# Moving the first four chunks' state updates of a fused linear-attention and ELU-MLP kernel into the second half of the first tile

## The chip, the cores and the metric

The kernel runs on one core of one Trainium2 chip. The metric is the device time of one execution in microseconds; the time of a version is the median of several executions.

## The reference

Decayed causal linear attention in blocks, for 4 batches, 8 heads, 768 positions and a head dimension of 64, followed by a two-layer network on the 3072 tokens of 512 features, with 2048 hidden features and ELU between the layers. Inputs and output are float32. Cut to what matters:

```python
for b in range(nb):                                   # blocks of the sequence
    intra = (qb @ kb.T * Dmask) @ vb                  # Dmask[i, j] = lam ** (i - j), i >= j
    inter = (qb * lam_pow) @ kv_state
    out[block b] = intra + inter
    kv_state = lam_block * kv_state + (kb * rev_pow).T @ vb
...
h = x @ w_in                                          # x: the heads of a token side by side
g = np.where(h > 0, h, np.exp(np.minimum(h, 0)) - 1)
y = g @ w_out
```

## The kernel before

The kernel uses blocks of 128 positions rather than 64. A chunk is one such block of one batch: with 6 blocks and 4 batches there are 24 chunks, numbered g = 4c + b. Chunks 0 to 3 are the first block of each batch, which have no state to read. The MLP runs over seven tiles of 4, 2, 4, 4, 4, 4 and 2 chunks (128 tokens per chunk), so tile 0 is chunks 0 to 3 (512 tokens).

Everything is ordered by hand (`manual_schedule`): the order in which the Python code emits instructions is the order of each engine's queue, and each engine works through its queue in order, waiting on what the tile framework finds it depends on.

For a chunk the attention part has these steps. `att_T` and `att_Te` transpose q and k on TensorE and copy them out (later chunks use a DMA transpose instead). `att_S` makes the score products into psS, `att_mask` multiplies them with the decay mask on VectorE into P (L323), `att_O` makes the output products from P and v (L337) and from q and the state (L345), and `att_X` writes the result as the MLP's input xt. For the state there are `att_kd`, the key decay kd = k times the per-head factors (L298 on VectorE or GpSimd, L296 on ScalarE), for two chunks at once; `att_U`, the update products from kd and v into psU (L383, 16 small matmuls for a pair of chunks); and `att_st`, which brings psU into the state st: for chunks 0 to 3 two plain copies per pair (L417, VectorE), later eight multiply-adds per pair (L421). So kd0, U0, st0 stand for chunks 0 and 1, and kd2, U2, st2 for chunks 2 and 3. The first reader of these states is `att_O` of chunks 4 and 5, at step B7, and of chunks 6 and 7.

The MLP has steps named (tile, n). `mm1` makes hidden feature block n of a tile, four matmuls into psH (L444), then exp into e (L473) and relu into r (L477) on ScalarE; `elu` combines them on VectorE into g (L490). For n = 2, 4 and 6 of tile 0 the relu is left out and VectorE does two instructions instead, m from e (L485) and g from m and psH (L488). `mm2` is one output product for one chunk of the tile and one block n, accumulated in psM (L541), copied out after n = 15 (L555, L557) and stored by SyncE's queue.

Tile 0 is special. Its 16 hidden blocks are steps A0 to A15; from A10 on each also holds two output products, of chunks 0 and 1. Steps B0 to B12 hold the other output products of tile 0, and between them the attention of chunks 4 to 7 (`visit`): chunk 4's transposes and kd4 at B1, its scores at B4, its output products at B7. Within a step the order is: `mm1`, then whatever `at` has put on this step, then `elu`, then the `mm2` of the step.

PSUM tiles are taken from tags with two slots each: "H" and "M" for psH and psM (in tile 0, the psH of even n below 9 use "M"), "S" for psT, psS, psO and psU. A new tile takes the slot of the tile before the last one of its tag, and its first writer waits until that tile has been read. The SBUF tags e and r have three slots, kd has two.

All loads with a cast from float32 to float16 are issued by GpSimd's queue, in the order of the list LOADS: q, k and v of the first chunks, then the slices wi0 to wi7 of W_in (128 KB each for wi0 and wi1, 256 KB for wi2 to wi6, 512 KB for wi7), the slices wo0 to wo4 of W_out (256 KB each for wo0 and wo1, else 512 KB), and q, k and v of later chunks in pairs. The entries ('kd', g) of the list are no loads: GpSimd itself computes kd of chunks g and g + 1 at that place of its queue. wi0 and wi1 hold hidden blocks 0 and 1, wi2 to wi6 blocks 2 to 11 in pairs, wi7 blocks 12 to 15; wo0 holds hidden blocks 0 and 1 for the second layer, wo1 blocks 2 and 3, wo2 to wo4 the rest in fours.

Of the kernel before, what the change touches and what calls it, by code (L numbers as in the profile page):

```python
# [15 lines left out]
def kernel(  # L16
# [12 lines left out]
    B, H, S, D = q.shape  # L29
# [82 lines left out]
        [cpool.tile([128, 2, HP, 128], FP16, name=f"st{j}_{i}") for i in range(2)]  # L112
        for j in range(B // 2)
    ]
    LOADS = [(0, 1, 'q'), (0, 1, 'k'), (1, 1, 'q'), (1, 1, 'k'), (2, 1, 'q'), (2, 1, 'k'), (3, 1, 'q'), (3, 1, 'k'), (0, 1, 'v'), (1, 1, 'v'), (2, 1, 'v'), (3, 1, 'v'), ('wi', 0), ('wi', 1), ('wi', 2), ('wi', 3), ('wi', 4), ('kd', 0), ('wi', 5), ('wi', 6), ('wo', 0), ('wi', 7), ('kd', 2), ('wo', 1), ('wo', 2), (4, 2), ('wo', 3), ('wo', 4), (6, 2), (8, 2), (10, 2), (12, 2), (14, 2), (16, 2), (18, 2), (20, 2), (22, 2)]

    def run_loads(items):
        for it in items:
            if it[0] == "wi":
                emit_wi(it[1])  # L120
            elif it[0] == "wo":
                emit_wo(it[1])
            elif it[0] == "kd":
                att_kd(it[1], 2, "p")
            else:
                emit_load(*it)

    run_loads(LOADS[:0])
    nc.gpsimd.iota(rel_i[:], pattern=[[1, 128]], base=0, channel_multiplier=-1)
    run_loads(LOADS[0:16])  # L130

# [447 lines left out]
    def at(s, f, *a, **k):  # L579
        run.setdefault(s, []).append(lambda: f(*a, **k))  # L580
# [66 lines left out]

    run_loads(LOADS[16:29])
    for s, g in zip([], (0, 2)):
        at(s, att_kd, g, 2)  # L650
    for s, g in zip([('A', 6), ('A', 9)], (0, 2)):
        at(s, att_U, g)
    for s, g in zip([('A', 7), ('A', 10)], (0, 2)):
        at(s, att_st, g)
        at(s, att_tmp, g + B)

# [39 lines left out]
    for s, a, b in [(('B', 2), 29, 30), ((1, 2), 30, 31), ((1, 14), 31, 32), ((2, 4), 32, 33), ((2, 12), 33, 34), ((3, 4), 34, 35), ((3, 12), 35, 36), ((4, 4), 36, 37)]:  # L696
        at(s, paced_load, s, LOADS[a:b])

# [51 lines left out]
```

## Time and profile before

| what | value |
|---|---|
| median of 7 executions | 212.71 us (212.54 to 213.73) |
| the profiled execution | 213.73 us, of which the span is 212.0 us |
| TensorE, matmuls busy | 201.9 us (95% of the span) |
| VectorE busy | 148.7 us (70%) |
| ScalarE busy | 127.1 us (60%) |
| GpSimd busy | 62.4 us (29%) |
| granted TensorE clock | 1.00 |
| steps A0 to A15 of tile 0 | 18.05 to 36.76 us of the span |
| kd of chunks 0, 1 and of 2, 3 on GpSimd | start 15.67 and 20.54, 2.05 and 2.16 us |
| U of chunks 0, 1 and of 2, 3 on TensorE | start 25.36 and 28.43 |
| state copies L417 on VectorE | start 28.50 and 31.86, two each, 0.69 us per copy |

The span runs from the first to the last instruction; the rest of an execution's time lies around it. A busy share is an average over stages with different limits, so the stages are looked at one by one. The TensorE clock was never throttled, so a difference in time is one of work or of waiting. All times inside the span are counted from its start.

### The profile page before, as it was taken

Reading aid. Unit: us, or ns where it says so; the run is one execution under the profiler, and the core shown is the slowest. Engines: PE = TensorE matmul, PEld = TensorE weight load, DVE = VectorE, ACT = ScalarE, POOL = GpSimd, SP = SyncE. Lnnn points to the kernel's source line nnn. Section 1 sums busy time; section 2 is a strip of 40 time slices with the busy share of each in tenths; the row PEclk is TensorE's granted clock in tenths of the full one; section 3 lists DMA queues with packets and bytes.
Section 4 is the critical chain, followed back from the end, with each engine's and each line's share of the span. In section 5 each row is a group of like instructions: output and inputs, shape, how many; then the busy total and the mean of one; then the engine's idle time right before and its main releaser. Section 6 shows DMA issues by size and latency. Waiting matters only on the chain.

```text
span 212.0 us, 4131 instructions
## 1 busy us (share of the span) xinstructions
PE 201.9 (95%) x1640; PEld 104.6 (49%) x1640; DVE 148.7 (70%) x241; ACT 127.1 (60%) x246; POOL 62.4 (29%) x71
## 2 busy tenths in 40 slices
PE   6786899999999999999999999999999999999994
PEld 2343344555865454544544544544544544466643
DVE  7662998477989999998698598677557634344321
ACT  5885778505694858666464666464567476675520
POOL 8999985400343352150600510600000000011000
PEclk9999999999999999999999999999999999999999
DMA  6999999999999999999699791599401111011112
GB/s 42 141 152 182 196 195 166 197 157 195 189 149 134 132 170 156 143 87 114 113 143 144 119 132 52 111 144 154 90 0 53 49 49 49 2 53 49 49 53 101
DMA packets 101284, 24.40 MB, mean 115 GB/s; under 512 B 93072, under 2 KB 98448, under 8 KB 101264
## 3 DMA queue, kind: packets, MB, share of 16 engines
q0 software_dynamic: 80912, 14.16, 86.6%
q1 hardware_dynamic: 20208, 9.90, 21.7%
q8 instruction: 13, 0.21, 0.4%
q10 hardware_dynamic: 144, 0.07, 0.1%
q14 instruction: 7, 0.06, 0.1%
HBM read 27.27 MB, written 6.29 MB: 158 GB/s over the span
## 4 chain that ended last, share of the span: by engine, by line
PE 79%; DVE 7%; POOL 5%; ACT 4%; DMA 3%; issue 1%; POOLq 0%; ACTq 0%
PE psM L541 36%; PE psH L444 28%; PE psH L462 5%; DVE g L490 3%; DMA wi<-in_moe_w_in_dram 3%; PE psO L337 2%; PE psS L311 2%; PE psO L345 2%; POOL qn L74 2%; POOL kn L74 2%; PE psM L521 2%; POOL vn L74 2%; ACT r L477 2%; DVE P L323 1%; ACT kd L296 1%
## 5 line engine op out<-in xcount | busy, mean ns | idle before, releaser
L541 PE MATMUL psM<-wo,g 128*128 128x512 f16 x368 | 94.0, 380 | 0.2 <-DVE g L490 0.2
L473 ACT ACTIVATE e<-psH 128x512 f32<-128x512 f32 x96 | 57.3, 598 | 61.4 <-PE psH L444 51.5
L490 DVE SCALAR_TENSOR_TENSOR g<-e,r 128x512 f16<-128x512 f32 x93 | 63.9, 702 | 38.2 <-ACT r L477 37.8
L444 PE MATMUL psH<-xt,wi 128*128 128x512 f16 (+2 forms) x324 | 81.2, 376 | 2.9 <-DMA wi<-in_moe_w_in_dram 1.7
L477 ACT ACTIVATE r<-psH 128x512 f16<-128x512 f32 x93 | 55.2, 594 | 0.0
L541 PEld LDWEIGHTS <-g 128*128 128x128 f16 x368 | 34.3, 98 | 38.5 <-DVE g L490 1.5
L444 PEld LDWEIGHTS <-wi 128*128 128x128 f16 x324 | 31.1, 98 | 40.8 <-DMA wi<-in_moe_w_in_dram 2.4
L323 DVE TENSOR_TENSOR P<-psS,mask 128x1024 f16<-128x1024 f32 (+1 forms) x28 | 28.7, 1066 | 5.7 <-PE psS L311 5.6
L691 POOL COPY pace<-g 1x1 f16<-1x1 f16 x7 | 2.3, 329 | 70.5 <-DVE g L490 70.5
L421 DVE SCALAR_TENSOR_TENSOR st<-st,up_p,psU 64x128 f16<-64x128 f16 x64 | 18.2, 346 | 0.1
L558 POOL DMA_DIRECT2D out_dram<-osb x2 | 1.1, 572 | 54.8 <-ACT osb L557 50.7
L366 DVE TENSOR_TENSOR xt<-psO,qs 128x1024 f16<-128x1024 f32 x10 | 12.2, 1223 | 6.7 <-PE psO L345 6.7
L462 PE MATMUL psH<-xt,wi 128*128 128x256 f16 x128 | 16.4, 273 | 0.0
L74 POOL DMA_DIRECT2D qn<-in_q_dram x14 | 15.3, 1092 | 3.2 <-issue 2.0
L74 POOL DMA_DIRECT2D kn<-in_k_dram x14 | 15.2, 1087 | 1.3 <-DMA kn<-in_k_dram 0.8
L74 POOL DMA_DIRECT2D vn<-in_v_dram x14 | 15.2, 1104 | 1.1 <-DMA wo<-in_moe_w_out_dram 1.1
L462 PEld LDWEIGHTS <-wi 128*128 128x128 f16 x128 | 12.3, 98 | 4.2
L557 ACT COPY osb<-psM 128x512 f32<-128x512 f32 x12 | 7.1, 592 | 12.2 <-PE psM L541 12.2
L337 PEld LDWEIGHTS <-vn 128*64 128x64 f16 x184 | 9.6, 109 | 4.9 <-issue 3.8
L337 PE MATMUL psO<-P,vn 128*64 128x128 f16 x184 | 11.5, 222 | 0.2
L345 PE MATMUL psO<-qT,st 128*64 128x128 f16 x160 | 10.0, 219 | 0.0
L345 PEld LDWEIGHTS <-st 128*64 128x64 f16 x160 | 8.9, 110 | 0.0
(58 smaller groups left out, 112.8 us busy)
## 6 DMA issues: line engine op xcount, KB each, us to landing
out_dram<-osb SPq DMA_DIRECT2D x21, 256.0 KB, 2.5
qn<-in_q_dram POOLq DMA_DIRECT2D x10, 256.0 KB, 6.9
kn<-in_k_dram POOLq DMA_DIRECT2D x10, 256.0 KB, 7.7
vn<-in_v_dram POOLq DMA_DIRECT2D x10, 256.0 KB, 9.0
wo<-in_moe_w_out_dram POOLq DMA_DIRECT2D x3, 512.0 KB, 13.1
wi<-in_moe_w_in_dram POOLq DMA_DIRECT2D x5, 256.0 KB, 7.0
qn<-in_q_dram POOLq DMA_DIRECT2D x4, 128.0 KB, 4.3
kn<-in_k_dram POOLq DMA_DIRECT2D x4, 128.0 KB, 4.3
```

The source lines that it names most:

```text
L74: nc.gpsimd.dma_start(out=dst, in_=src[b : b + n, :, rows].rearrange("b h p d -> p (b h) d"))
L323: nc.vector.tensor_tensor(out=P[:, :, c], in0=s[:, :, c], in1=(mask if g < B else mask1)[:, :, c], op=ALU.mult,)
L337: nc.tensor.matmul(po[r, i, hp, :], lhsT=v_of(g + i, 2 * hp + hh), rhs=P[:, hh, hp, :], start=True, stop=(c == 0), skip_group_check=True,)
L345: nc.tensor.matmul(po[r, i, hp, :], lhsT=st[(g + i) % B // 2][c % 2][:, (g + i) % 2, hp, r], rhs=qT[g + i][:, hp, :], start=False, stop=Tr ...
L366: nc.vector.tensor_tensor(out=dst, in0=po[:, :, c], in1=qs[:, c].unsqueeze(1).broadcast_to([128, n, w, 128]), op=ALU.mult,)
L421: nc.vector.scalar_tensor_tensor(out=new[r, :, hp, r], in0=old[r, :, hp, r], scalar=up_p[r, hp : hp + 1], in1=pu[r, :, hp, :], op0=ALU.mul ...
L444: nc.tensor.matmul(pH[:, lo:hi], lhsT=wi[:, kk, j * 128 : (j + 1) * 128], rhs=xt[t][:, kk, lo:hi], start=(kk == 0), stop=(kk == HP - 1),)
L462: nc.tensor.matmul(pH[:, x * MT : (x + 1) * MT], lhsT=wi[:, kk, j * 128 : (j + 1) * 128], rhs=xt[t][:, kk, :], start=(kk == 0), stop=(kk = ...
L473: nc.scalar.activation(e[:], pH[:], AF.Exp)
L477: nc.scalar.activation(r[:], pH[:], AF.Relu)
L490: nc.vector.scalar_tensor_tensor(out=g, in0=e[:], scalar=-1.0, in1=r[:], op0=ALU.add, op1=ALU.min)
L541: nc.tensor.matmul(pm[:], lhsT=gt[t][:, n, i * L : (i + 1) * L], rhs=wo_t[wo_at[n][0]][:, wo_at[n][1], :], start=(n == 0), stop=(n == NF - 1),
```

## The change

Three things move, none is added or removed. In LOADS, the two key decays on GpSimd go behind the last slice of W_in: kd0 from behind wi4 to behind wi7, and kd2 from behind wi7 to behind wo1. With this wi7 comes ahead of wo0. The update products go from A6 and A9 to B0 and B2, and the state copies from A7 and A10 to B1 and B3. The calls of `att_tmp` that go along do nothing in this version.

```diff
-    LOADS = [..., ('wi', 4), ('kd', 0), ('wi', 5), ('wi', 6), ('wo', 0), ('wi', 7), ('kd', 2), ('wo', 1), ('wo', 2), (4, 2), ...]
+    LOADS = [..., ('wi', 4), ('wi', 5), ('wi', 6), ('wi', 7), ('kd', 0), ('wo', 0), ('wo', 1), ('kd', 2), ('wo', 2), (4, 2), ...]
...
-    for s, g in zip([('A', 6), ('A', 9)], (0, 2)):
+    for s, g in zip([('B', 0), ('B', 2)], (0, 2)):
         at(s, att_U, g)
-    for s, g in zip([('A', 7), ('A', 10)], (0, 2)):
+    for s, g in zip([('B', 1), ('B', 3)], (0, 2)):
         at(s, att_st, g)
         at(s, att_tmp, g + B)
```

More of the change, by code (lines that the diff above doesn't have):

```diff
@@ L114 @@
     ]
-    LOADS = [(0, 1, 'q'), (0, 1, 'k'), (1, 1, 'q'), (1, 1, 'k'), (2, 1, 'q'), (2, 1, 'k'), (3, 1, 'q'), (3, 1, 'k'), (0, 1, 'v'), (1, 1, 'v'), (2, 1, 'v'), (3, 1, 'v'), ('wi', 0), ('wi', 1), ('wi', 2), ('wi', 3), ('wi', 4), ('kd', 0), ('wi', 5), ('wi', 6), ('wo', 0), ('wi', 7), ('kd', 2), ('wo', 1), ('wo', 2), (4, 2), ('wo', 3), ('wo', 4), (6, 2), (8, 2), (10, 2), (12, 2), (14, 2), (16, 2), (18, 2), (20, 2), (22, 2)]
+    LOADS = [(0, 1, 'q'), (0, 1, 'k'), (1, 1, 'q'), (1, 1, 'k'), (2, 1, 'q'), (2, 1, 'k'), (3, 1, 'q'), (3, 1, 'k'), (0, 1, 'v'), (1, 1, 'v'), (2, 1, 'v'), (3, 1, 'v'), ('wi', 0), ('wi', 1), ('wi', 2), ('wi', 3), ('wi', 4), ('wi', 5), ('wi', 6), ('wi', 7), ('kd', 0), ('wo', 0), ('wo', 1), ('kd', 2), ('wo', 2), (4, 2), ('wo', 3), ('wo', 4), (6, 2), (8, 2), (10, 2), (12, 2), (14, 2), (16, 2), (18, 2), (20, 2), (22, 2)]
     def run_loads(items):
```

## The prediction

> **What bounds the kernel now.** I read the page's first part, then the table of busy time by stretches, then the chain that ended last, then the timelines of the engines around the moved work.
>
> ```profile
> PE 201.9 (95%) x1640; PEld 104.6 (49%) x1640; DVE 148.7 (70%) x241; ACT 127.1 (60%) x246; POOL 62.4 (29%) x71
> ```
>
> TensorE is busy 95% of the span, so only places where it waits can be won. Stretches of 4 us (start:end, length, then busy us of PE, PEld, DVE, ACT, POOL):
>
> ```profile
> 22.00:26.00 4.00, 3.20 (x30) 1.39 (x29) 3.93 (x6) 3.19 (x6) 4.00 (x5) 1.00 1.31 195
> 30.00:34.00 4.00, 3.72 (x18) 1.56 (x16) 3.92 (x7) 3.15 (x6) 2.46 (x3) 1.00 2.03 170
> 38.00:42.00 4.00, 4.00 (x45) 2.31 (x42) 1.83 (x3) 1.93 (x2) 1.42 (x2) 1.00 1.41 196
> 42.00:46.00 4.00, 4.00 (x65) 2.34 (x62) 2.42 (x3) 0.00 (x0) 0.00 (x0) 1.00 2.41 158
> ```
>
> In the first half of tile 0 (steps A) VectorE is full and TensorE has gaps; in the second half (steps B, from about 37 us) TensorE is full and VectorE half idle. The chain says the same (start, us, what):
>
> ```profile
> 21.23 2.02 DVE g L490
> ...
> 27.89 0.69 DVE g L488
> 28.58 0.59 DVE st L417
> 29.20 0.69 DVE st L417
> 29.93 0.70 DVE g L490
> ...
> 31.31 0.50 ACT r L477
> 31.85 1.02 PE psH L444 x4
> ...
> 36.76 1.29 PE psM L541 x6
> 38.05 0.89 PE psT L224 x16
> ...
> 41.54 0.55 PE psS L311 x16
> 42.09 2.70 PE psM L541 x12
> ```
>
> From 21.23 to 30.63 it runs through VectorE, a state copy (L417) in it, and from 31.85 to 57.77 through TensorE without a break.
>
> ```profile
> 20.54 2.16 POOL L298 TENSOR_TENSOR kd<-kn,ks 128x1024 f16<-128x1024 f16 x1
> 24.41 1.02 PE L444 MATMUL psH<-xt,wi 128*128 128x512 f16 x4 [0.80 <-DVE g L488]
> 37.91 0.69 DVE L490 SCALAR_TENSOR_TENSOR g<-e,r 128x512 f16<-128x512 f32 x1 [0.60 <-ACT r L477]
> ```
>
> The g of 21.23 takes 2.02 us instead of 0.69 and ends 0.55 after GpSimd's kd; the wait of step A6 at 24.41 is its consequence.
>
> **What the Trainium skill says.** "SBUF — State Buffer", section "Who interferes with whom": a VectorE instruction with two SBUF inputs contends with a GpSimd instruction that reads SBUF, one in a two-port mode with any GpSimd instruction; the first to issue holds the pair for its whole instruction. The trace agrees: g (L490, e and r both in SBUF) took 2.02 us beside kd, and m (L485, one SBUF source) 0.40, 0.63 and 0.97 us in the chain, the longer two while GpSimd issued loads. "DMA: Bandwidth & Descriptors", section "Queues, rings and completion order": within a ring, descriptors are consumed in order. The landings of the weights agree, below.
>
> **The change part by part.**
>
> *GpSimd's order.* After wi4 (15.67) came kd0, wi5, wi6, wo0, wi7, kd2, wo1; now wi5, wi6, wi7, kd0, wo0, wo1, kd2. One weight load takes 0.70 to 0.79 us there, kd0 1.85 from its start to that of the next. So kd0 starts at 15.67 + 0.77 + 0.77 + 0.79 = 18.0 and wo0 at 19.85, before VectorE's first g (20.25): kd0 stays free. kd2 starts at 19.85 + 0.70 + 0.76 = 21.3, hence beside the second g (21.23 to 21.92). It waits for that, then holds the pair to about 23.55; m2, queued behind g1, waits for it. Then m2 ends at 23.95, g2 at 24.6 (24.36 before). The lock moves from g1 to m2 and costs 0.25 us here. Bounds: if m2 gets in ahead of kd2, g2 ends at 23.05, but g3, with two SBUF inputs, is blocked instead; if kd2 lingers, g2 ends at 24.75.
>
> *The weights' landings.* Issue to landing was 7.5 us for wo0 (19.05) and 9.4 for wi7 (19.75):
>
> ```profile
> wi<-in_moe_w_in_dram POOLq DMA_DIRECT2D x1, 512.0 KB, 9.4
> wo<-in_moe_w_out_dram POOLq DMA_DIRECT2D x1, 256.0 KB, 7.5
> ```
>
> So the landings were wi5 23.9, wi6 25.3, wo0 26.55, wi7 29.15, wo1 30.35: about 1.3 us for each 256 KB, a backlog served in order. Issuing earlier brings nothing; order does. Now wi7 lands at 25.3 + 2.6 = 27.9 (nobody needs it before A12) and wo0 at 29.15. The first output product (psM, step A10) started at 29.68: from 29.2 on wo0 is its floor. wo1 (30.4) and wo2 (32.9) stay ahead of their users; k4 landed at 36.7, and its transposes still come after that.
>
> *State copies (L417).* Four by 0.69 us leave VectorE's queue in A. g7, which ended at 30.63, now ends near 29.4, so exp and relu (ACT) at A10 no longer wait, and A12's wait goes. What is late next is A11's buffer (relu of A9, behind m6) and wo0. With the first output product at 29.2 to 29.35, TensorE's own work from there to the end of A15 is 5 first-layer groups plus the A10 to A14 output pairs: 5 x 0.864 + 5 x 0.43 = 6.48 us. A15 ends at 35.7; with a wait of 0.3 at A11 at 36.0. Before: 36.76. **Gain 0.74 to 1.06 us; I take 0.95.**
>
> *Update products (L383).* In A they lay beside TensorE's waits; in B nothing covers them. Each is 0.25 us in the chain at 45.80, and 0.37 from start to the next start in A (28.43 to 28.80). Two: 0.5 to 0.74; I take **0.6 lost**.
>
> *VectorE and the PSUM slots in B.* Tag "S" has two slots. The order was U0, U2, T4, S4, S5; it is now U0, T4, U2, S4, S5. So U2 needs st0 done and S5 needs st2 done. Counted from A15's end: VectorE's last g ends at 38.60 - 36.76 = 1.84; st0 (1.40 for its pair) 3.24; kd4 (L298, 1.22) 4.46; st2 5.86. TensorE reaches U2 at 0.43 + 0.25 + 0.86 + 0.89 + 0.86 = 3.29, hardly late, and S5 at 3.29 + 0.25 + 0.86 + 0.86 + 0.28 = 5.54. S5 waits until about 5.92: **0.4 lost**, with all TensorE work behind it. Bounds: 0 if U's longer 0.37 delays TensorE by as much, 0.6 if a copy is slowed. The mask of chunk 5 ends at about 8.3, and O(5) comes at about 9.2: covered. kd4's slot needs U0 only, long done. The two DVE copies as such (2.8 us) lie in VectorE's idle time in B. SP's queue and GpSimd's loads in B stay in their order.
>
> *Sum:* -0.95 + 0.6 + 0.4 = +0.05 us. The profiled execution took 213.73 us with a span of 212.0, thus 1.73 around it and 1.02 over the median; I put the sum on the median: **212.7 us**. The ends of the terms, with U's two prices tied to S5's wait, give -0.25 to +0.6.
>
> **The rivals.** About 0.64 us (0.3%) is what a measurement of this kernel can tell from no change.
>
> *B swallows the moved work (faster).* If S5 doesn't wait on st2 and the update products cost nothing net, the gain of A stays: 212.71 - 1.06 = 211.65; with the products paid, 212.1. For it: VectorE is under half busy from 38 to 42. Against: TensorE's chain has no gap there for 0.5 us of added products. Chance of more than 0.64: 0.18.
>
> *wo0 decides at A10 (slower).* wo0 is now issued at 19.85 behind 512 KB more. If it lands later than 29.15, every later tenth comes off A's gain, as A11 stands behind it on TensorE and nothing after A10 waits elsewhere. At 30.2 the gain is gone: 30.2 + 6.48 = 36.7. Then products and S5's wait remain, 1.0 lost: 213.7. The limit of 0.64 is passed from 29.85 on. Against it: the even landings. For it: a landing of 10.3 us after issue is in the range of what other loads of the queue show (wo1 7.7, wo2 9.5, k4 11.4). The same 1.0 would follow if kd2's lock put m2 so late that A6 starts near 25.5. Together 0.28.
>
> *It doesn't do what it says:* if kd2 didn't collide at all, VectorE would lead in A, but wo0's floor keeps the gain at 1.06, so this changes only 0.1 us.
>
> **How the numbers follow.** Nothing measurable 0.54, faster 0.18, slower 0.28. The likeliest case's own range is 212.45 to 213.3; to leave out 1 in 10 at either end it stretches to the faster rival without its extreme, 211.9, and to the slower one, 213.8.
>
> **What would show each step.** Right: TensorE's gap before A12 gone; one m (L485) near 2 us in place of the long g, or a g3 of that length; wo0 landing near 29.2, with the first psM product just after; A15 ending near 35.8; a new wait of psS (L311) on st (L417) of about 0.4 us near 41.5; chunk 4's and 5's O products (L337) at the same time as before, 44.8, within 0.5. Wrong: a wait of L541 on the wo load well beyond 29.5, a wait at the first psO of B, or a TensorE chain of B that starts earlier by 1 us and stays so.

## The result, and the profile after

The changed kernel takes 213.86 us in the median of 13 executions (213.62 to 214.71), the kernel before 212.61 us in the median of 34. The ratio is 1.0061, with a 95% interval of 1.005 to 1.0073: about 1.3 us slower.

The two profiled executions don't show this: the span was 212.0 us before and 211.9 after. The execution of the kernel before that was profiled had taken 213.73 us, 1.1 over its own median, while the one profiled after (213.71) was as long as its timed ones. A second profile of the kernel before took 213.93 us; a third, with 212.67 us and a span of 210.8, has the usual length. It is called "before, third profile" here, and the changed kernel is compared with it.

The engines' totals after, from the page:

```profile
PE 203.4 (96%) x1640; PEld 105.5 (50%) x1640; DVE 150.6 (71%) x241; ACT 127.4 (60%) x246; POOL 62.5 (29%) x71
```

Three of the stretches of 4 us shown of before, now after (start:end, length, busy us of PE, PEld, DVE, ACT, POOL):

```profile
22.00:26.00 4.00, 2.73 (x13) 1.17 (x12) 3.93 (x5) 2.75 (x6) 4.00 (x4) 1.00 1.32 204
30.00:34.00 4.00, 4.00 (x20) 1.86 (x19) 2.51 (x4) 3.45 (x8) 2.46 (x3) 1.00 2.11 170
38.00:42.00 4.00, 4.00 (x53) 2.06 (x50) 3.63 (x6) 1.93 (x2) 1.63 (x2) 1.00 1.48 195
```

The same stretches of before, third profile (two of them):

```profile
22.00:26.00 4.00, 3.93 (x33) 1.71 (x31) 3.93 (x7) 3.13 (x6) 4.00 (x5) 1.00 1.31 199
30.00:34.00 4.00, 4.00 (x20) 1.82 (x19) 3.90 (x7) 3.66 (x8) 2.44 (x3) 1.00 2.00 167
```

The change did what it set out to do: VectorE has room from 30 to 34 us (2.51 against 3.90 busy) and takes the copies in from 38 to 42. But in a usual execution of the kernel before TensorE was not short of work from 30 to 34: it was full at 4.00. And from 22 to 26 it now works 2.73 us in place of 3.93. The chain that ended last, after (start, us, what):

```profile
18.86 2.83 DVE g L490 x2
21.70 2.05 DVE m L485
...
23.77 0.70 DVE g L488
...
24.52 4.64 PE psH L444 x20
29.15 0.55 PE psM L541 x2
...
35.78 0.43 PE psM L541 x2
36.21 0.37 PE psU L383 x16
36.59 0.97 PE psM L541 x4
37.55 0.89 PE psT L224 x16
38.45 0.86 PE psM L541 x4
39.31 0.37 PE psU L383 x16
39.68 1.83 PE psM L541 x8
41.52 0.55 PE psS L311 x16
```

And of before, third profile:

```profile
21.63 1.22 DVE m L485
...
23.62 1.02 PE psH L444 x4
24.65 0.37 PE psU L383 x16
25.02 2.70 PE psH L444 x12
27.71 0.37 PE psU L383 x16
28.09 0.97 PE psH L444 x4
...
35.56 1.29 PE psM L541 x6
36.86 0.89 PE psT L224 x16
37.75 2.59 PE psM L541 x12
40.34 0.55 PE psS L311 x16
```

Both chains hang on m2 (L485) until step A6, and then on TensorE without a break up to chunk 4's scores (psS), 40.34 before and 41.52 after: 1.18 us. This is made up as follows.

- A6 starts 0.90 later (24.52 against 23.62).
- The two update products are no longer in A. Each took 0.37 us there, and the group behind it 0.11 more than its matmuls alone (2.70 for 12 of them against 12 x 0.216 = 2.59, 0.97 for 4 against 4 x 0.216 = 0.86): 0.95 less for both.
- TensorE waits 0.27 more in A: 0.16 in the 20 matmuls from A6 on (4.64, against 1.02 for the first four and 16 x 0.216 = 3.46 for the rest), and 0.1 at A10's two output products (0.55 for the two, elsewhere 0.43). So A15 ends 0.22 later (35.78 against 35.56).
- In B the products are 0.37 each again, and the output products behind each take 0.11 and 0.10 more (0.97 against 0.86, 1.83 against 8 x 0.216 = 1.73): 0.95.

The sum is 0.22 + 0.95 = 1.17. The products cost the same in both places, so moving them comes to nothing. What the change costs is A6's 0.90 and the 0.27 of waiting behind it. The spans differ by 1.1.

The two waits after A6, in the timelines of VectorE and of TensorE's weight loads (PEld), after:

```profile
25.66 0.69 DVE L488 TENSOR_TENSOR g<-m,psH 128x512 f16<-128x512 f16 x1
26.40 2.25 PEld L444 LDWEIGHTS <-wi 128*128 128x128 f16 x11 [0.28 <-issue]
29.09 0.11 PEld L541 LDWEIGHTS <-g 128*128 128x128 f16 x2 [0.43 <-DMA wo<-in_moe_w_out_dram]
```

The psH of A8 takes the slot of A4's, which g4 (L488) reads until 26.35; A8 starts right behind it. With the products gone from A, TensorE has caught up with the late VectorE. At A10 the weight load waits for wo0 until 29.09. TensorE was still at work for most of that wait, so it cost 0.1.

Why A6 is late, in the timelines of VectorE and GpSimd (start, us, engine, line, operation), first before, third profile, then after:

```profile
20.54 2.01 POOL L298 TENSOR_TENSOR kd<-kn,ks 128x1024 f16<-128x1024 f16 x1
21.63 1.21 DVE L485 TENSOR_SCALAR m<-e 128x512 f16<-128x512 f32 x1 [0.89 <-ACT e L473]
```

```profile
21.21 2.24 POOL L298 TENSOR_TENSOR kd<-kn,ks 128x1024 f16<-128x1024 f16 x1
21.62 2.12 DVE L485 TENSOR_SCALAR m<-e 128x512 f16<-128x512 f32 x1
```

m2 starts at the same time in both, which is a coincidence: before, it waited for e, and after, for the two g ahead of it, the first of which took 2.23 us. It takes 0.42 us when nothing holds it; it ends 0.29 us after GpSimd's kd2 in each. kd2 ends at 22.55 before and 23.45 after, and this 0.90 is A6's delay.

### The profile page after: what moved, and what is told of

Read it like the earlier page. It is cut to its first block, busy times and chain, and to the rows that moved or that the text cites. A ratio compares the mean times of both kernels' runs of the same rounds, so it can differ in the third digit from the quotient of the medians.

```text
span 211.9 us, 4128 instructions
## 1 busy us (share of the span) xinstructions
PE 203.4 (96%) x1640; PEld 105.5 (50%) x1640; DVE 150.6 (71%) x241; ACT 127.4 (60%) x246; POOL 62.5 (29%) x71
## 4 chain that ended last, share of the span: by engine, by line
PE 76%; DVE 13%; POOL 3%; DMA 2%; ACT 2%; issue 1%; POOLq 0%; ACTq 0%
PE psM L541 34%; PE psH L444 26%; PE psH L462 5%; DVE g L490 5%; PE psO L337 3%; DMA vn<-in_v_dram 2%; PE psS L311 2%; DVE P L323 2%; DVE st L421 2%; POOL qn L74 2%; DVE xt L366 2%; PE psO L345 2%; PE psM L521 2%; POOL kn L74 2%; ACT kd L296 1%
## 5 line engine op out<-in xcount | busy, mean ns | idle before, releaser
L569 PE MATMUL psW<-ones 128*128 128x512 f16 x20 | 8.4, 520 | 1.1 <-DVE ones L55 1.1
```

## The experiments

Each is compared with the kernel before on the same chip; the time is the median of the executions, the ratio has its 95% interval. Three theories: **1**, GpSimd's key decays hold VectorE's port at the wrong moment (1a: only the decays do; 1b: the issue of loads does too); **2**, the products and copies in the second half cost the time; **3**, wo0 lands too late behind wi7.

**The kernel before again.** No edit.

> The kernel before, unchanged, profiled once more. In the trace on which the prediction rests, the first hidden block (A0) starts at 18.05 us, after 1.7 us of waiting for the first W_in slice, and that execution took 213.73 us, 1.1 us over the median; in the trace of the changed kernel A0 starts at 16.6 us. Theory: the execution traced was an unlucky one, and a typical one has a span of about 210.9 us, starts A0 near 16.6 us and has the key decay of chunks 2 and 3 (GpSimd, 20.5 to 22.7 us) beside other VectorE instructions than the second g. Rival: the start is the kernel's own, A0 starts near 18 us again. Time: ratio 1.000.

212.55 us, ratio 1.0007 (0.9992 to 1.0023). The profiled execution took 213.93. A0 started at 16.75, but wi2 landed late, at 21.1, and A15 ended at 36.84. So the late start of A0 was that one execution's; how late a W_in slice lands differs from one execution to the next.

**The load list alone.**

```diff
-    LOADS = [..., ('wi', 4), ('kd', 0), ('wi', 5), ('wi', 6), ('wo', 0), ('wi', 7), ('kd', 2), ('wo', 1), ...]
+    LOADS = [..., ('wi', 4), ('wi', 5), ('wi', 6), ('wi', 7), ('kd', 0), ('wo', 0), ('wo', 1), ('kd', 2), ...]
```

> Only the load list of the changed kernel (key decays behind wi7 and wo1); update products and state copies stay at A6, A7, A9 and A10. Theory 1, port lock: the decays on GpSimd now lie beside the first g (18.9 us) and m2 (21.6 us) and block VectorE there, so this alone costs most of the 1.25 us: 213.4 to 214.2. Theory 2, the products and the states in the second half cost it: this is like the kernel before, 212.4 to 212.8. Theory 3, wo0 behind wi7: 213 or more, with a wait on wo0 of over 0.5 us at A10.

213.80 us, 1.0041 (1.002 to 1.0062): the load list alone is as slow as the whole change. wo0 was not what A10 waited for. The chain of this run goes through m2 too:

```profile
21.61 2.06 DVE m L485
...
24.43 1.02 PE psH L444 x4
...
31.82 1.02 PE psH L444 x4
...
36.73 1.29 PE psM L541 x6
```

A6 is as late as after. A15 ends at 36.73, 0.95 later than after, because the products, 0.95 us for both, are still in A. With VectorE late, TensorE also waits before A12: it starts at 31.82, where the work ahead of it was done at 31.42 (0.40 us; 0.03 in before, third profile). The changed kernel has no such wait at A12, but the two of 0.16 and 0.1 shown above. So in these traces moving the copies wins back 0.1 us.

**The moves alone.**

```diff
-    for s, g in zip([('A', 6), ('A', 9)], (0, 2)):
+    for s, g in zip([('B', 0), ('B', 2)], (0, 2)):
         at(s, att_U, g)
-    for s, g in zip([('A', 7), ('A', 10)], (0, 2)):
+    for s, g in zip([('B', 1), ('B', 3)], (0, 2)):
```

> Only the moved update products and state copies (B0 to B3); the load list is that of the kernel before. Theory 1, port lock: no loss, 212.0 to 212.8, as VectorE is relieved in A and TensorE pays 0.9 in B. Theory 2: slower by about 1 us, 213.4 to 214.0. Theory 3: like theory 1.

212.96 us, 1.0016 (1.0 to 1.0031). Above the range of theory 1, far below that of theory 2; the interval is 0 to 0.66 us. The products cost as much in A as in B, so they don't explain a loss. In the profiled execution (213.42 us, longer than the median) TensorE, with the products gone from A, waits 0.19 us before A8 and 0.16 before A11 instead. That would account for 0.3 us, but one trace doesn't show it.

**kd0 back behind wi4**, the rest as changed.

```diff
-    ('wi', 4), ('wi', 5), ('wi', 6), ('wi', 7), ('kd', 0), ('wo', 0), ('wo', 1), ('kd', 2)
+    ('wi', 4), ('kd', 0), ('wi', 5), ('wi', 6), ('wi', 7), ('wo', 0), ('wo', 1), ('kd', 2)
```

> The changed kernel, but with the key decay of chunks 0 and 1 back behind wi4, where it lies ahead of the first g; wi7 still ahead of wo0, and the decay of chunks 2 and 3 still behind wo1. Theory 1, port lock: only one of two blocked VectorE instructions is left, some 0.4 to 0.9 us of the loss goes: 212.9 to 213.4. Theory 2 and 3: no change against the changed kernel, 213.6 to 214.0.

213.62 us, 1.0046 (1.0027 to 1.0066): only 0.24 less than changed, above the range of theory 1. kd0's place is not the cause: the first g took 2.27 us here too, beside loads alone, and m2 2.12 beside kd2.

**kd2 one place later**, nothing else.

```diff
-    ('wi', 7), ('kd', 2), ('wo', 1), ('wo', 2)
+    ('wi', 7), ('wo', 1), ('kd', 2), ('wo', 2)
```

> The kernel before with one edit: the key decay of chunks 2 and 3 changes places with wo1 on GpSimd, so it starts at about 21.3 us in place of 20.5. Theory 1 (port): in timed executions of the kernel before, m2 gets past VectorE's queue before this decay takes the port, or waits for its earlier end; 0.75 us later it holds m2 and with it step A6: slower by 0.5 to 1.0 us, 213.1 to 213.6. Theory 3 (order of the weights): no change, 212.5 to 212.7.

213.72 us in the median of three executions (213.60 to 214.02), 1.0053 (1.0035 to 1.0071). This one exchange gives 1.1 us, most of the loss and more than expected. The granted clock was 0.66 in the profiled execution, which is left out of the median; its VectorE and GpSimd timelines show the collision, but not its price:

```profile
21.22 2.03 POOL L298 TENSOR_TENSOR kd<-kn,ks 128x1024 f16<-128x1024 f16 x1
21.46 2.08 DVE L485 TENSOR_SCALAR m<-e 128x512 f16<-128x512 f32 x1
```

**wi7 ahead of wo0**, the kernel before otherwise.

```diff
-    ('wi', 6), ('wo', 0), ('wi', 7), ('kd', 2)
+    ('wi', 6), ('wi', 7), ('wo', 0), ('kd', 2)
```

> The kernel before with one edit: wi7 is issued ahead of wo0; the key decays stay where they were in GpSimd's queue, behind wi4 and behind both of these loads. Theory 3, wo0's landing: slower by 0.5 us or more with a wait on wo0 at A10. Theory 1b, port held by the issue of loads too (in the run with kd0 back the first g took 2.27 us beside three W_in loads, against 1.2 to 1.3 beside two): the first g ends near 20.9 us in place of 20.1, the second g falls under the decay that starts at 20.5, and the time is 0.5 to 1.0 us longer: 213.1 to 213.6. Theory 1a, only the decays hold the port: 212.5 to 212.7.

212.91 us, 1.0005 (0.9993 to 1.0017), with single executions from 212.5 to 213.7. Inconclusive on 1a and 1b: the first g took 1.47 us here. Theory 3's loss of 0.5 us or more is not there, but wo0 doesn't come quite in time either. In the profiled execution (213.49 us, with A1 late behind its W_in slice) the weight load of A10 waits for it:

```profile
29.65 0.11 PEld L541 LDWEIGHTS <-g 128*128 128x128 f16 x2 [0.51 <-DMA wo<-in_moe_w_out_dram]
```

The work ahead on TensorE was done at 29.47, so this cost 0.18 us.

**kd2 behind wo4**, the rest as changed.

```diff
-    ('wo', 1), ('kd', 2), ('wo', 2), (4, 2), ('wo', 3), ('wo', 4), (6, 2)
+    ('wo', 1), ('wo', 2), (4, 2), ('wo', 3), ('wo', 4), ('kd', 2), (6, 2)
```

> The changed kernel, but the key decay of chunks 2 and 3 behind wo4, at about 27 us in GpSimd's queue, where VectorE has time to spare. Theory 1: m2 isn't held for 2 us, A6 starts at about 23 us in place of 24.5, but wo0 at 29.15 and the products in the second half remain: 212.6 to 213.2, at least 0.6 under the changed kernel. Theory 3: 213.6 to 214.0, as with the changed kernel.

213.46 us, 1.0049 (1.0027 to 1.007), single executions from 212.9 to 215.1: 0.4 less than changed, not the 0.6 or more expected, and with intervals that overlap. In the profiled execution (212.91 us) m2 is free (0.53 us, at 21.03) and TensorE goes without a break from A2 to A10. There it meets theory 3 after all:

```profile
28.27 0.60 PE L541 MATMUL psM<-wo,g 128*128 128x512 f16 x2 [1.24 <-DMA wo<-in_moe_w_out_dram]
```

**Both decays on VectorE**, at A12 and A14, the rest as changed.

```diff
-    ('wi', 7), ('kd', 0), ('wo', 0), ('wo', 1), ('kd', 2), ('wo', 2)
+    ('wi', 7), ('wo', 0), ('wo', 1), ('wo', 2)
...
-    for s, g in zip([], (0, 2)):
+    for s, g in zip([('A', 12), ('A', 14)], (0, 2)):
         at(s, att_kd, g, 2)
```

> The changed kernel with both key decays on VectorE, at A12 and A14 (1.22 us each, where VectorE had 0.6 us free in each step of 1.3 us), none on GpSimd; loads follow each other without them. Theory 1a, decays hold the port: 212.2 to 213.0, as with the decay last. Theory 1b, the loads' issue holds it too: the first g is still held to about 20.4 us, but nothing holds m2: 212.4 to 213.0 as well. Theory 3: 213.6 to 214.0.

213.36 us, 1.0031 (1.002 to 1.0043): above the range of theory 1 again. The same picture: nothing holds the first g (0.69 us) and m2 (0.43), and A10 waits 1.24 us, until 28.61. The profile puts that down to the g of block 9, which A10's products (block 0) don't read; wo0 landed at 28.57, so it is the load.

**The kernel before, a third profile.**

> The kernel before, unchanged: a third profile, as both profiled executions so far took 213.7 to 213.9 us where the timed ones take 212.6. Theory: in a timed execution the third W_in slice (wi2) lands early enough (near 19.1 us) for m2 to get through VectorE before the decay of chunks 2 and 3 takes the port, or just as it does; then A15 ends near 35.6 us in place of 36.8 and the span is near 210.9. If the profile is again over 213.4 us it shows the late landing again, and this stays open.

212.67 us, span 210.8: the one shown above. A15 ended at 35.56, as expected; m2 did not get ahead of kd2, though: it was held, but for 0.8 us instead of 1.7.

**kd2 one place earlier.**

```diff
-    ('wi', 7), ('kd', 2), ('wo', 1)
+    ('kd', 2), ('wi', 7), ('wo', 1)
```

> The kernel before with the key decay of chunks 2 and 3 one place earlier, ahead of wi7 (start near 19.75 us in place of 20.5). Theory 1 (it matters beside which VectorE instruction the decay falls): it now holds the second g from about 20.2 to 21.7 us, m2 comes near 22.7: slower by 0.2 to 0.8 us, 212.8 to 213.4. Rival (later is worse, as the weights behind it are late): faster or the same, 212.2 to 212.6.

213.00 us, 1.0008 (0.9994 to 1.0022), with single executions from 212.4 to 213.8: neither side's gain or loss is shown. The second g was held as expected:

```profile
20.37 2.01 DVE L490 SCALAR_TENSOR_TENSOR g<-e,r 128x512 f16<-128x512 f32 x1 [1.01 <-ACT r L477]
```

but kd2 also ended 0.74 earlier, and A6 started at 23.53, as in the kernel before. In this trace what counts is the end of kd2 plus the VectorE work still queued ahead of g2, and not beside which instruction it falls. But ten of the 20 executions took over 213.1 us (12 of 55 of the kernel before), and the profiled one, with 212.48, is not of these: what makes them longer is not shown.

**kd2 behind wo4, wo0 ahead of wi7, kd0 behind wi4.**

```diff
-    ('wi', 4), ('wi', 5), ('wi', 6), ('wi', 7), ('kd', 0), ('wo', 0)
+    ('wi', 4), ('kd', 0), ('wi', 5), ('wi', 6), ('wo', 0), ('wi', 7)
```

> As the run with the decay of chunks 2 and 3 behind wo4 (213.46 us; A10 waited 1.24 us for wo0 there), but wo0 is issued ahead of wi7 again and the decay of chunks 0 and 1 is back behind wi4; products and states stay in the second half. Theory (with the port free, wo0's landing is the next bound): the wait at A10 goes, 212.0 to 212.7, 0.8 to 1.3 us faster than that run. Rival (the products and states in the second half make up the rest): 213.0 to 213.5.

213.45 us, 1.002 (1.0004 to 1.0036): in the rival's range, not the theory's. Nine of the 20 executions took 212.7 to 213.0 us, the others 213.3 to 214.9. The wait at A10 is gone (the first output product at 27.18), but the profiled execution (213.66, of the longer ones) has a new one, and it is not the products'. VectorE and TensorE:

```profile
26.45 5.00 DVE L490 SCALAR_TENSOR_TENSOR g<-e,r 128x512 f16<-128x512 f32 x4
30.78 1.02 PE L444 MATMUL psH<-xt,wi 128*128 128x512 f16 x4 [1.44 <-ACT r L477]
```

kd2 ran from 27.0 to 29.0, beside these four g, which take 0.69 each when free and 2.7 together; relu behind them was late, and A12 waited for it.

**Both decays on VectorE, wo0 ahead of wi7.**

```diff
-    ('wi', 6), ('wi', 7), ('wo', 0), ('wo', 1)
+    ('wi', 6), ('wo', 0), ('wi', 7), ('wo', 1)
```

> As the run with both key decays on VectorE (213.36 us; A10 waited 1.24 us), but with wo0 ahead of wi7 again. Same theory and rival: 211.9 to 212.6, or 213.0 to 213.4.

212.20 us, 0.9972 (0.9957 to 0.9988): faster than both kernels, and 1.16 us under the run with the same decays and wo0 behind wi7, which is close to the 1.24 waited there. TensorE's first output product at A10:

```profile
27.68 0.59 PE L541 MATMUL psM<-wo,g 128*128 128x512 f16 x2
```

There is no wait before it. A15 ends at 34.59, 0.97 earlier than in before, third profile, which is about the price of the products that left A; in B they take it again, and chunk 4's scores start at 40.33 (40.34 before). The profiled execution, at 212.55, was one of the longer of this kernel, so its trace doesn't show where the 0.5 us of the medians (212.20 against 212.69) is won.

## Why the prediction was wrong, point by point

- **The base.** This is the step that failed: the gain of 0.95 in A, from "A12's wait goes" and "Before: 36.76", with "I put the sum on the median". The end of A15 after was forecast at 35.7 to 36.0 and is 35.78. But 36.76 belonged to an execution 1.1 us longer than usual, and the extra lay in the very stage that the change touches: A0 started at 18.05 rather than 16.6, and the second g was held for 2.02 us. In before, third profile, A15 ends at 35.56, and the wait at A12, 0.45 us in the first profile (31.40 to 31.85), is 0.03 us. The gain of 0.95 was a loss of 0.22. The terms of B, forecast at 0.6 + 0.4 = 1.0, came to 0.95 + 0 (below), so this step makes the whole miss.
- **The port.** That kd2 would collide with m2 was right, and so was the end of g2 (24.6 forecast, 24.47 measured). "The lock moves from g1 to m2 and costs 0.25 us" was a mis-sized term: 0.90 in the traces, and kd2 one place later costs 1.1 us in timed executions by itself. It was sized against a g1 that was held for 2.02 us in the first profile, but took 0.69 in the second and 0.68 in the third. "kd0 stays free" failed as well: the first g came at 18.86, not 20.25, and took 2.23 us. That the second g still began close to its forecast (21.02 against 21.23), right ahead of kd2, was luck: the earlier start of the first and its hold cancelled. The run with kd0 back shows only that kd0's place mattered little (0.24 us); the first g was held there too.
- **wo0.** The landing at 29.15 was about right (the weight load of A10 waited until 29.09), and as A6 was late, it cost TensorE 0.1 us. The weight slices landed in the order of their issue in every trace, as the prediction took it. wo0 is the next bound: 1.24 us where the port is free. The rival without a collision had it as the bound; its gain of 0.1 was 0.4 in the medians (kd2 behind wo4), not clear of noise.
- **The update products.** 0.95 in place of 0.6: 0.37 each and 0.1 in the group behind each. The 0.25 was read where other small products come first, and the 0.37 leaves out the group behind. "In A they lay beside TensorE's waits" failed too: they cost the same 0.95 in A, so their move is neither gain nor loss. The forecast put the gain in A down to the copies; in the traces what leaves A is the products' own time.
- **S5 behind st2.** No wait is shown: st2 ended at 41.61 and the second half of the scores came after that, as the longer products had brought TensorE there later. The bound of 0 given for this case held. That this term was 0.4 too high and the products' 0.35 too low, so that the two nearly cancel, is luck.
- **The rivals.** The slower one had the sign and the size (213.7) but the wrong mechanism; its aside, kd2's lock on m2 with A6 at 25.5, names the right one with an A6 that is 1 us too late (it started at 24.52). The faster one needed products that cost nothing in B, and TensorE was full there.

What stays open is why W_in slices land later in some executions (wi0 at 18.00 us in the first profile of the kernel before and at 16.31 in the third, wi2 at 21.05 in the second and at 19.88 in the third), and what else than kd holds the first g.

## What to carry to other kernels

Before costing a change from one profiled execution, set its time beside the median; if the difference is as large as the effects in question, find the stage where it lies, and take another profile if it is the stage that the change touches. An instruction on GpSimd that shares VectorE's port is priced by when it ends, set against the VectorE work that the next TensorE step needs: here 0.7 us later cost 1.1 us. The update products cost TensorE 0.95 us in A and in B alike, so moving such work between two stages in which the engine is full wins nothing by itself. Where decays of this kind fit into VectorE's own idle time (1.22 us against 2.05), put them there, and then order the weight loads by first use.

## What was not expected of the hardware

The first g (two SBUF inputs, 0.69 us when free) took 2.27 us beside W_in and W_out loads that GpSimd merely issued, with no decay near it, in the run with kd0 back, and 1.19 in the kernel before, profiled again. In the run with kd2 behind wo4 and wo0 first, GpSimd's queue was the same up to there as in the kernel before, and it took 0.69. In four traces (the second and third of the kernel before, the moves alone, wi7 ahead of wo0) it began at 18.67 to 18.96 and ended at 20.14 or 20.15 each time, about 0.4 us after GpSimd began to issue a load; with kd0 back it ended at 20.90, again 0.4 us after one began. This points to the issue of loads as what holds it; that it is, and by what rule, these runs don't show.
